# Linear attention and a two-layer perceptron on one core: the second layer of two token tiles as seven block products

## Chip, core, metric

The kernel runs on one NeuronCore of a Trainium2 chip. The metric is the device time of one execution in microseconds, as the median of several runs of the same program; smaller is better. Beside the times there is one profiled execution, whose trace gives start and duration of the instructions of each engine: TensorE (PE for matrix products, PEld for the loads of their stationary operand), VectorE (DVE), ScalarE (ACT), GpSimd (POOL) and SyncE (SP, which here only issues DMAs).

## What is computed

Batch 8, 8 heads, sequence 576, head width 64: 4608 tokens of width 512. The attention has no score matrix: softmax of q over the head width, softmax of k over the sequence, then two small products. The result is the input of two dense layers with a leaky rectifier between them.

```
q_s = softmax(q, over head width);  k_s = softmax(k, over the sequence)
kv  = einsum('bhsd,bhse->bhde', k_s, v)
x   = einsum('bhsd,bhde->bhse', q_s, kv)   -> 4608 x 512
h   = x @ w_in                             (512 x 2048)
g   = maximum(0.01 * h, h)
out = g @ w_out                            (2048 x 512), float32
```

## The kernel before

**Tiles.** The 4608 tokens are cut into nine token tiles of 512 (`NT = 9`, `TT = 512`). `xT` holds x transposed (bf16), `w_in_sb` and `w_out_sb` hold the two weights in bf16 with 128 rows of the summed index on the partitions. The order of all instructions is written out by hand; each engine works through its own list in order.

**One token tile t = 1 to 8 (lines 866 to 890).** First layer: for each of the 16 blocks j of 128 hidden channels, `layer1` (line 562) makes four matmuls with a moving operand of 512 tokens into one PSUM bank `ph`, and `leaky` (line 571) turns the bank on ScalarE into a bf16 tile `gj`. Second layer: for each of the four groups `tsub` of 128 tokens, `layer2` (line 583) makes 16 matmuls, one for each j, with a stationary block of 128 x 128 of `gj` and a moving operand of 512 columns of `w_out_sb`, all summed in one bank `pout`. `store` (line 575) copies the bank to `out_sb` (ScalarE for tiles up to 7, VectorE in tile 8) and issues two DMAs of 64 rows each from SP (line 580). The last group of tile 8 is made in two parts of 384 and 128 columns, and of each part one of the two DMAs is issued from ScalarE's queue.

**PSUM.** `psB_pool` has six banks under one tag, used in turn by `ph` and others; `psO_pool` has two for `pout`.

**Work around it.** Attention for batch b + 1 is prepared on VectorE, ScalarE, GpSimd and by DMAs while tile b is multiplied. It is hung into the loops by hooks: `at(t, u, fn)` notes it, `run(t, u)` emits it, with u below 16 for the blocks j of the first layer and 16 + 4 tsub + j // 4 for the second layer. The last attention work, that of batch 7, is emitted at (6, 23). So tiles 7 and 8 have nothing but the two layers. The SBUF pools of the attention (`raw`, `ke`, `qe`, `mx`, `small`, `qT`) stay allocated to the end, though.

**Start.** `wake` (line 370) makes a few matmuls on float32 zeros, `k_max_pe` (line 381) a transposition and `k_all_pe` (line 396) small products in float32, all within the first 12 us. They are the only float32 matmuls of the program.

Of the kernel before, what the change touches and what calls it, by code (L numbers as in the profile page):

```python
# [7 lines left out]

FP32 = mybir.dt.float32
BF16 = mybir.dt.bfloat16  # L10
AF = mybir.ActivationFunctionType
ALU = mybir.AluOpType
AX = mybir.AxisListType
# [6 lines left out]
L = 64  # L20
# [5 lines left out]
def kernel(  # L26
# [9 lines left out]
    nc = tc.nc  # L36
# [3 lines left out]
    B, H, S, D = q.shape  # L40
    C = H * D
    T = B * S
    Cm, F = moe_w_in.shape
    F2, O = moe_w_out.shape
    assert Cm == C and F2 == F and L * R == S and HL * 2 == H

    P = 128
    NB = C // P
    NF = F // P
    TT = 512  # L50
    NT = T // TT
# [3 lines left out]
    const_pool = ctx.enter_context(tc.tile_pool(name="const", bufs=1))  # L55
    w_pool = ctx.enter_context(tc.tile_pool(name="wts", bufs=1))
    xT_pool = ctx.enter_context(tc.tile_pool(name="xT", bufs=1))
    raw_pool = ctx.enter_context(tc.tile_pool(name="raw", bufs=6))
    ke_pool = ctx.enter_context(tc.tile_pool(name="ke", bufs=2))
    qe_pool = ctx.enter_context(tc.tile_pool(name="qe", bufs=2))  # L60
    mx_pool = ctx.enter_context(tc.tile_pool(name="mx", bufs=1))
    small_pool = ctx.enter_context(tc.tile_pool(name="small", bufs=3))
    qT_pool = ctx.enter_context(tc.tile_pool(name="qT", bufs=2))
    g_pool = ctx.enter_context(tc.tile_pool(name="gsb", bufs=10))
    osb_pool = ctx.enter_context(tc.tile_pool(name="osb", bufs=4))

    psB_pool = ctx.enter_context(tc.tile_pool(name="psB", bufs=6, space=bass.MemoryType.PSUM))
    psO_pool = ctx.enter_context(tc.tile_pool(name="psO", bufs=2, space=bass.MemoryType.PSUM))
    BANK_TAG = "bank2k"
# [30 lines left out]
    nc.gpsimd.memset(zero, 0.0)  # L100
    ident = const_pool.tile([P, P], BF16)
    make_identity(nc, ident)
    identf = const_pool.tile([P, P], FP32)
    make_identity(nc, identf)
    warm = const_pool.tile([P, 1], BF16)
    nc.scalar.activation(out=warm, in_=ident[:, 0:1], func=AF.Exp)
    gate = const_pool.tile([P, 1], FP32)

    w_in_sb = w_pool.tile([P, NB, F], BF16)
    w_out_sb = w_pool.tile([P, NF, O], BF16)  # L110
    xT = xT_pool.tile([P, NB, T], BF16)


    XH, X8, XE = (slice(0, 7), slice(9, 16)), slice(7, 9), slice(16, 20)
    qe1 = const_pool.tile([P, XE.stop, P], BF16, name="qe1")
    vb2 = [const_pool.tile([P, R, 2, 2, D + 2], BF16, name=f"vb{i}") for i in range(2)]
# [85 lines left out]
    def k_exp(b, hs):  # L202
        nc.scalar.activation(  # L203
            out=st[b]["ke"][:, :, hs].rearrange("p r h d -> p h r d"),
            in_=st[b]["k"][:, hs],
            func=AF.Exp,
        )
# [36 lines left out]
    def q_first(b, rs):  # L244
# [3 lines left out]
        for gg in range(2):  # L248
# [5 lines left out]
            for h in range(2):  # L254
                for r in range(n):
                    nc.scalar.activation(
                        out=st[b]["qe"][:, rs.start + r, 2 * gg + h],
                        in_=st[b]["q"][:, 2 * gg + h, rs.start + r],
                        func=AF.Exp,
                        bias=nmax[:, 2 * gg + h, r : r + 1],  # L260
# [47 lines left out]
    def q_exp(b, rs, hs=ALLH):  # L308
        nc.scalar.activation(  # L309
            out=q_cols(b, rs, hs).rearrange("p r h d -> p h r d"),  # L310
            in_=st[b]["q"][:, hs, rs],
            func=AF.Exp,
        )
# [140 lines left out]
    def q_keep(eng, b, r0, n, gs=slice(0, 4)):  # L454
        o, i = st[b]["qT"][:, gs, r0 : r0 + n], st[b]["ps", r0][:, gs]
        if eng is nc.scalar:
            eng.copy(out=o, in_=i)
        else:
            eng.tensor_copy(out=o, in_=i)
# [100 lines left out]
    def layer1(j, ph, c0, n, part=slice(0, 4), first=True, last=True):  # L560
        for cb in range(NB)[part]:
            nc.tensor.matmul(  # L562
                ph,
                lhsT=w_in_sb[:, cb, j * P : (j + 1) * P],
                rhs=xT[:, cb, c0 : c0 + n],
                start=(cb == 0 and first),
                stop=(cb == NB - 1 and last),
            )

    def leaky(o, ph):  # L570
        nc.scalar.activation(out=o, in_=ph, func=AF.Prelu, alpha=LEAKY_SLOPE)  # L571

    out_r = out.rearrange("(b l r) o -> b r l o", b=B, r=R)

    def store(row0, pout, copy=nc.vector.tensor_copy, os=slice(0, O), issue=(nc.sync, nc.sync)):
        out_sb = osb_pool.tile([P, O], FP32, name="out_sb")[:, os]
        copy(out=out_sb, in_=pout)  # L577
        for i in range(2):
            b, c = divmod(row0 + i * L, S)
            issue[i].dma_start(out=out_r[b, c // L, :, os], in_=out_sb[i * L : (i + 1) * L])  # L580

    def layer2(pout, g_sb, tsub, j, os=slice(0, O)):
        nc.tensor.matmul(  # L583
            pout,
            lhsT=g_sb[j // 2][:, j % 2, tsub * P : (tsub + 1) * P],
            rhs=w_out_sb[:, j, os],
            start=(j == 0),
            stop=(j == NF - 1),
        )
# [4 lines left out]
    def at(t, u, *fns):  # L594
        while t > 0 and u >= 32:
            t, u = t + 1, u - 32
        hooks.setdefault((t, u), []).extend(fns)

    def run(t, u):
        for fn in hooks.pop((t, u), ()):  # L600
            fn()
# [161 lines left out]
    for t in range(3, B - 1):  # L763
        b = t + 1
# [11 lines left out]
            at(t, 5, lambda b=b: load_all(b + 2))  # L776


    def g_tiles():
        return [g_pool.tile([P, 2, TT], BF16, name="gj") for _ in range(NF // 2)]  # L780

    g_sb = g_tiles()

    def begin(js, parts):
# [16 lines left out]
    def end_act(j, ph, half):  # L801
# [4 lines left out]
    t2 = (  # L806
        lambda: q_transpose(0, 6, 2, psO_pool, "pout"),
        lambda: q_keep(nc.vector, 0, 6, 2),
    )
# [38 lines left out]
    for j in range(0, NF, 2):  # L848
        if j == 0:
            ph = ahead  # L850
        else:
            ph = psB_pool.tile([P, 2, 256], FP32, name="ph", tag=BANK_TAG)
            end_pe(j, ph, 1, slice(0, 4), True)
        end_act(j, ph, 1)
    pout = [psO_pool.tile([P, O], FP32, name="pout", tag="pout") for _ in range(2)]
# [8 lines left out]
        store(tsub * P, pout[tsub])  # L864

    for t in range(1, NT):
        g_sb = []
        for j in range(NF):
            ph = psB_pool.tile([P, TT], FP32, name="ph", tag=BANK_TAG)
            layer1(j, ph, t * TT, TT)  # L870
            if j % 2 == 0:
                g_sb.append(g_pool.tile([P, 2, TT], BF16, name="gj"))
            leaky(g_sb[j // 2][:, j % 2], ph)
            run(t, j)
        for tsub in range(NTS):
            row0 = t * TT + tsub * P
            if row0 == T - P:
                for os, copy in ((slice(0, 384), nc.scalar.copy), (slice(384, O), nc.vector.tensor_copy)):
                    po = psB_pool.tile([P, os.stop - os.start], FP32, name="pout2", tag=BANK_TAG)
                    for j in range(NF):  # L880
                        layer2(po, g_sb, tsub, j, os)
                    store(row0, po, copy, os, (nc.sync, nc.scalar))
                break
            po = psO_pool.tile([P, O], FP32, name="pout", tag="pout")
            for j in range(NF):
                layer2(po, g_sb, tsub, j)
                if j == NF - 1:
                    store(row0, po, nc.scalar.copy if t < NT - 1 else nc.vector.tensor_copy)
                if j % 4 == 3:
                    run(t, 16 + 4 * tsub + j // 4)  # L890
    assert not hooks, list(hooks)
# [30 lines left out]
```

## Time and profile before

| what | value |
|---|---|
| time, median of 3 runs | 281.36 us (281.27 to 281.75) |
| span of the profiled execution, first to last instruction | 279.3 us |
| PE busy | 272.3 us, 97% of the span |
| PEld busy | 133.1 us, 48% |
| DVE, ACT, POOL busy | 158.4, 159.6 and 49.5 us |
| granted TensorE clock | 1.000 |
| HBM read, written | 36.70 MB, 9.44 MB |

The runs give the time of whole executions; the profiled execution's own time is its span and a little around it that the trace does not show: 281.36 - 279.3 = 2.1 us if it ran like the median run. A line of a profile gives source line, engine, operation, the tiles written and read, shape and type, count, then busy time in us and the mean duration of one instruction in ns. Starts and durations in a timeline are in us from the first instruction. The duration of a matmul includes the way through the array, which the next matmul does not wait for: the spacing of matmuls in a row is read from starts, not from durations.

### The profile page before, as it was taken

The page shows a single profiled execution, that of the slowest core. Times are in us where ns is not written, and L with a number is a line of the kernel's source. Part 1 is how long each engine was busy: PE and PEld are TensorE (multiplying, and loading weights), DVE is VectorE, ACT ScalarE, POOL GpSimd, SP SyncE. Part 2 cuts the span into 40 slices and gives each one's busy share as a digit, 9 for nine tenths or more (in the row PEclk, how much of TensorE's full clock was granted, in tenths as well). Part 3 has the DMA queues.
Part 4 walks back from the last instruction along what each step waited for, and adds up shares of the span by engine and source line. Part 5 has one row for each costly group of instructions (what it writes and reads, how often), then busy time and mean ns, then how long its engine had stood idle before and what let it go on. Part 6 is the DMA issues. An engine that isn't in the chain of part 4 may idle for free.

```text
span 279.3 us, 4849 instructions
## 1 busy us (share of the span) xinstructions
PE 272.3 (97%) x1927; PEld 133.1 (48%) x1954; DVE 158.4 (57%) x228; ACT 159.6 (57%) x283; POOL 49.5 (18%) x55
## 2 busy tenths in 40 slices
PE   8999999999999999999999999999999999999994
PEld 3488644444444454445444544454444444444443
DVE  3986986999999949957794688543700000000021
ACT  4977573783598458744675458644844464146400
POOL 2957460258003004000400140000000000000000
PEclk9999999999999999999999999999999999999999
DMA  7999999977993696099309930333033300330033
GB/s 253 326 209 325 246 242 306 403 269 200 300 410 139 116 405 227 2 307 361 78 9 311 347 77 2 84 77 75 1 87 75 75 1 2 75 75 0 2 75 75
DMA packets 40006, 46.45 MB, mean 166 GB/s; under 512 B 18736, under 2 KB 23344, under 8 KB 39984
## 3 DMA queue, kind: packets, MB, share of 16 engines
q1 hardware_dynamic: 36320, 41.82, 48.3%
q0 software_dynamic: 3504, 4.20, 8.7%
q8 instruction: 15, 0.25, 0.3%
q10 hardware_dynamic: 160, 0.13, 0.2%
q14 instruction: 7, 0.06, 0.1%
HBM read 36.70 MB, written 9.44 MB: 165 GB/s over the span
## 4 chain that ended last, share of the span: by engine, by line
PE 93%; DVE 3%; DMA 2%; issue 1%; ACT 0%; SPq 0%; ACTq 0%
PE pout L583 44%; PE ph L562 44%; DMA k_raw<-in_k_dram 2%; PE po L476 2%; DVE t L157 1%; PE pokv L338 1%; PE pkv L338 1%; PE pkv L416 0%; DVE k_raw L407 0%; ACT ke L203 0%; ACT gj L571 0%; DVE kmax L157 0%; DVE kd L431 0%; DVE kr L391 0%; PE pokv L476 0%
## 5 line engine op out<-in xcount | busy, mean ns | idle before, releaser
L583 PE MATMUL pout<-w_out_sb,gj 128*128 128x512 bf16 (+2 forms) x574 | 126.3, 373 | 1.2 <-issue 0.3
L562 PE MATMUL ph<-xT,w_in_sb 128*128 128x512 bf16 (+1 forms) x631 | 126.1, 357 | 0.5
L571 ACT ACTIVATE gj<-ph 128x512 bf16<-128x512 f32 x144 | 82.2, 601 | 26.0 <-PE ph L562 25.1
L562 PEld LDWEIGHTS <-w_in_sb 128*128 128x128 bf16 x640 | 62.3, 98 | 62.1 <-issue 0.2
L583 PEld LDWEIGHTS <-gj 128*128 128x128 bf16 x592 | 56.5, 98 | 65.6 <-issue 0.2
L577 ACT COPY out_sb<-pout 128x512 f32<-128x512 f32 (+1 forms) x29 | 16.8, 580 | 68.3 <-PE pout L583 43.1
L577 DVE COPY out_sb<-pout 128x512 f32<-128x512 f32 (+1 forms) x8 | 4.8, 637 | 70.8 <-PE pout L583 70.8
L215 POOL CAST vb<-v_raw 128x1152 bf16<-128x1152 f32 x13 | 21.1, 1650 | 81.4 <-DMA v_raw<-in_v_dram 81.4
L318 DVE TENSOR_REDUCE qsum<-qe 128x36 f32<-128x2304 bf16 (+5 forms) x13 | 20.0, 1542 | 10.5 <-ACT qe L309 10.4
L203 ACT ACTIVATE ke<-k_raw 128x2304 bf16<-128x2304 f32 (+2 forms) x13 | 18.0, 1384 | 8.4 <-DVE k_raw L195 8.0
L325 DVE TENSOR_TENSOR qe<-qe,qrec 128x2304 bf16<-128x2304 bf16 (+5 forms) x13 | 21.5, 1657 | 0.5
L242 DVE TENSOR_REDUCE qmax<-q_raw 128x36 f32<-128x2304 f32 (+5 forms) x13 | 20.0, 1539 | 0.1
L309 ACT ACTIVATE qe<-q_raw 128x2304 bf16<-128x2304 f32 (+5 forms) x13 | 17.1, 1315 | 4.3 <-POOL q_raw L301 3.4
L195 DVE TENSOR_TENSOR k_raw<-k_raw,kall 128x1152 f32<-128x1152 f32 (+2 forms) x10 | 18.0, 1820 | 0.3
L301 POOL TENSOR_TENSOR q_raw<-q_raw,qmax 128x512 f32<-128x512 f32 (+3 forms) x7 | 11.8, 1682 | 20.6 <-DMA q_raw<-in_q_dram 13.8
L499 ACT CAST xT<-po 128x448 bf16<-128x448 f32 (+3 forms) x34 | 14.4, 515 | 1.1 <-PE po L476 1.1
L301 DVE TENSOR_TENSOR q_raw<-q_raw,qmax 128x2304 f32<-128x2304 f32 (+1 forms) x6 | 14.0, 2332 | 0.2
L157 DVE TENSOR_TENSOR t<-t 128x256 f32<-128x256 f32 (+2 forms) x22 | 13.2, 599 | 0.7
L358 DVE RECIPROCAL krec<-pokv 128x2 f32<-128x2 f32 x8 | 1.3, 166 | 21.3 <-PE pokv L476 21.3
L157 DVE TENSOR_TENSOR t<-k_raw 128x512 f32<-128x512 f32 (+1 forms) x11 | 11.2, 1016 | 1.2 <-DMA k_raw<-in_k_dram 1.0
L370 PE MATMUL pout<-zero 128*128 128x512 f32 (+3 forms) x18 | 9.6, 659 | 1.0 <-POOL zero L100 1.0
L338 PEld LDWEIGHTS <-ke 64*64 64x64 bf16 x504 | 5.9, 107 | 3.4 <-issue 3.0
(68 smaller groups left out, 105.3 us busy)
## 6 DMA issues: line engine op xcount, KB each, us to landing
out_dram<-out_sb SPq DMA_DIRECT2D x70, 128.0 KB, 2.6
q_raw<-in_q_dram SPq DMA_DIRECT2D x6, 1152.0 KB, 8.8
v_raw<-in_v_dram SPq DMA_DIRECT2D x6, 1152.0 KB, 11.5
k_raw<-in_k_dram SPq DMA_DIRECT2D x5, 1152.0 KB, 6.2
k_raw<-in_k_dram SPq DMA_DIRECT2D x6, 576.0 KB, 6.1
v_raw<-in_v_dram SPq DMA_DIRECT2D x4, 576.0 KB, 7.6
w_in_sb<-in_moe_w_in_dram POOLq DMA_DIRECT2D x7, 256.0 KB, 7.0
w_out_sb<-in_moe_w_out_dram POOLq DMA_DIRECT2D x6, 256.0 KB, 9.3
```

The costliest lines, as they stand in the source:

```text
L157: nc.vector.tensor_tensor(out=o, in0=i0, in1=i1, op=ALU.max)
L195: eng.tensor_tensor(out=ks, in0=ks, in1=st[b]["kall"][:, hs].unsqueeze(2).to_broadcast([P, n, R, D]), op=ALU.subtract,)
L203: nc.scalar.activation(out=st[b]["ke"][:, :, hs].rearrange("p r h d -> p h r d"), in_=st[b]["k"][:, hs], func=AF.Exp,)
L215: eng.tensor_copy(out=o, in_=i)
L242: nc.vector.tensor_reduce(out=o, in_=st[b]["q"][:, hs, rs], axis=AX.X, op=ALU.max)
L301: eng.tensor_tensor(out=qs, in0=qs, in1=st[b]["qmax", rs.start, hs.start].unsqueeze(3).to_broadcast([P, m, n, D]), op=ALU.subtract,)
L318: nc.vector.reduce_sum(out=qsum, in_=q_cols(b, rs, hs), axis=AX.X)
L325: nc.vector.tensor_tensor(out=qes if out is None else out, in0=qes, in1=st[b]["qrec", rs.start, hs.start].unsqueeze(3).to_broadcast([P, n, ...
L562: nc.tensor.matmul(ph, lhsT=w_in_sb[:, cb, j * P : (j + 1) * P], rhs=xT[:, cb, c0 : c0 + n], start=(cb == 0 and first), stop=(cb == NB - 1 ...
L571: nc.scalar.activation(out=o, in_=ph, func=AF.Prelu, alpha=LEAKY_SLOPE)
L577: copy(out=out_sb, in_=pout)
L583: nc.tensor.matmul(pout, lhsT=g_sb[j // 2][:, j % 2, tsub * P : (tsub + 1) * P], rhs=w_out_sb[:, j, os], start=(j == 0), stop=(j == NF - 1),)
```

## The change

For tiles 7 and 8 (`FAST`) the second layer is computed as a 2 x 2 block product by a scheme of Strassen's kind. The 512 tokens are cut into two halves of 256 (`M2`), the 2048 hidden channels into even and odd blocks of 128 (`N2` = 8 blocks each), the 512 outputs into two halves of 256 columns (`H2`). The plain block product needs eight products of a 256 x 1024 with a 1024 x 256 block. The new one needs seven, made of 16 matmuls with 256 moving columns each, and sums of blocks before and after:

- `late_begin`, hung at (6, 24), gives up the attention's pools and allocates the new tiles in their place (`reuse_waits="tile"`: a write to a new tile waits for whoever last used that memory). It makes the sums of weight blocks t1 to t4 (128 x 2048 each: t3 on GpSimd, the others on VectorE) and a float32r copy of the block b22 on GpSimd. float32r is a four-byte type that the matmul takes in place of float32.
- `fast_layer1` replaces the first layer's loop of these tiles. The matmuls are the same; for odd j the bank is turned by two ScalarE instructions of 256 columns, one into a bf16 tile, one into the float32r tile a22. After every fourth j the sums s1, s2, s4 (VectorE) and s3 (GpSimd) of 128 x 512 are made.
- `fast_layer2` makes the products a11 b11 and a12 b21 in bf16, and s2 t2, s3 t3, s1 t1, a22 t4 and s4 b22 with both operands in float32r. ScalarE copies the first product out; VectorE adds each of the others, read from PSUM, to a float32 sum in SBUF, eleven instructions a tile. `put` issues the output DMAs. In tile 8 (`last`) the left half of the first 256 tokens is put after the second product, the other 256 tokens after the sixth, the right half of the first 256 tokens after the seventh; there the second DMA of each pair goes through ScalarE's queue, all others through SP.

The special ending of the last group (384 and 128 columns) is gone with the old loop for these tiles.

```diff
+F32R = mybir.dt.float32r
...
-    raw_pool = ctx.enter_context(tc.tile_pool(name="raw", bufs=6))
-    ke_pool = ctx.enter_context(tc.tile_pool(name="ke", bufs=2))
-    qe_pool = ctx.enter_context(tc.tile_pool(name="qe", bufs=2))
-    mx_pool = ctx.enter_context(tc.tile_pool(name="mx", bufs=1))
-    small_pool = ctx.enter_context(tc.tile_pool(name="small", bufs=3))
-    qT_pool = ctx.enter_context(tc.tile_pool(name="qT", bufs=2))
     g_pool = ctx.enter_context(tc.tile_pool(name="gsb", bufs=10))
     osb_pool = ctx.enter_context(tc.tile_pool(name="osb", bufs=4))
+    front = ctx.enter_context(ExitStack())
+    raw_pool = front.enter_context(tc.tile_pool(name="raw", bufs=6))
+    ke_pool = front.enter_context(tc.tile_pool(name="ke", bufs=2))
+    qe_pool = front.enter_context(tc.tile_pool(name="qe", bufs=2))
+    mx_pool = front.enter_context(tc.tile_pool(name="mx", bufs=1))
+    small_pool = front.enter_context(tc.tile_pool(name="small", bufs=3))
+    qT_pool = front.enter_context(tc.tile_pool(name="qT", bufs=2))
...
+    FAST = (7, 8)
+    N2, M2, H2 = NF // 2, TT // 2, O // 2
+    E1, E2 = slice(0, H2), slice(H2, O)
+    late = {}
+    def late_begin():
+        front.close()
+        pool = ctx.enter_context(tc.tile_pool(name="late", bufs=1, reuse_waits="tile"))
+        w = w_out_sb.rearrange("p (m two) o -> p m two o", two=2)
+        b11, b12, b21, b22 = w[:, :, 0, E1], w[:, :, 0, E2], w[:, :, 1, E1], w[:, :, 1, E2]
+        for n in ("b22", "t1", "t2", "t3", "t4"):
+            late[n] = pool.tile([P, N2, H2], F32R, name=n)
+        late["b11"], late["b21"] = w[:, :, 0, E1], w[:, :, 1, E1]
+        for n in ("s1", "s2", "s3", "s4", "a22"):
+            late[n] = pool.tile([P, N2, M2], F32R, name=n)
+        for n in ("e1", "u2", "u3", "u4"):
+            late[n] = pool.tile([P, 2, H2], FP32, name=n)
+        full = lambda n: late[n].bitcast(FP32)
+        nc.gpsimd.tensor_tensor(out=late["t3"], in0=b22, in1=b12, op=ALU.subtract)
+        nc.vector.tensor_tensor(out=late["t1"], in0=b12, in1=b11, op=ALU.subtract)
+        nc.vector.tensor_tensor(out=late["t2"], in0=b22, in1=full("t1"), op=ALU.subtract)
+        nc.vector.tensor_tensor(out=late["t4"], in0=b21, in1=full("t2"), op=ALU.subtract)
+        nc.gpsimd.tensor_copy(out=late["b22"], in_=b22)
+    def fast_layer1(t):
+        even = [g_pool.tile([P, 2, TT], BF16, name="gj") for _ in range(N2 // 2)]
+        odd = [g_pool.tile([P, 4, M2], BF16, name="gj") for _ in range(N2 // 4)]
+        for j in range(NF):
+            m = j // 2
+            ph = psB_pool.tile([P, TT], FP32, name="ph", tag=BANK_TAG)
+            layer1(j, ph, t * TT, TT)
+            if j % 2 == 0:
+                leaky(even[m // 2][:, m % 2], ph)
+            else:
+                leaky(odd[m // 4][:, m % 4], ph[:, 0:M2])
+                leaky(late["a22"][:, m], ph[:, M2:TT])
+            if j % 4 == 3:
+                ms, lo = slice(m - 1, m + 1), m // 2
+                a11, a21 = even[lo][:, :, 0:M2], even[lo][:, :, M2:TT]
+                a12 = odd[m // 4][:, m % 4 - 1 : m % 4 + 1]
+                part = lambda n: late[n][:, ms]
+                read = lambda n: late[n][:, ms].bitcast(FP32)
+                nc.gpsimd.tensor_tensor(out=part("s3"), in0=a11, in1=a21, op=ALU.subtract)
+                nc.vector.tensor_tensor(out=part("s1"), in0=a21, in1=read("a22"), op=ALU.add)
+                nc.vector.tensor_tensor(out=part("s2"), in0=read("s1"), in1=a11, op=ALU.subtract)
+                nc.vector.tensor_tensor(out=part("s4"), in0=a12, in1=read("s2"), op=ALU.subtract)
+            run(t, j)
+        return (lambda m: even[m // 2][:, m % 2, 0:M2]), (lambda m: odd[m // 4][:, m % 4])
+    def fast_layer2(t, a11, a12, last):
+        of = lambda n: (lambda m: late[n][:, m])
+        def product(a, w, pool=psB_pool, tag=BANK_TAG, each=False):
+            ps = [pool.tile([P, H2], FP32, name="pp", tag=tag) for _ in range(2)] if each else None
+            if not each:
+                both = pool.tile([P, 2, H2], FP32, name="pp", tag=tag)
+                ps = [both[:, 0], both[:, 1]]
+            for i in range(2):
+                for m in range(N2):
+                    nc.tensor.matmul(
+                        ps[i],
+                        lhsT=a(m)[:, i * P : (i + 1) * P],
+                        rhs=w(m),
+                        start=(m == 0 and (each or i == 0)),
+                        stop=(m == N2 - 1 and (each or i == 1)),
+                    )
+            return ps if each else both
+        def add(o, ps, e):
+            nc.vector.tensor_tensor(out=o, in0=ps, in1=e, op=ALU.add)
+        out1, out2 = ([osb_pool.tile([P, O], FP32, name="out_sb") for _ in range(2)] for _ in range(2))
+        def put(i, half, cols, issue=(nc.sync, nc.sync)):
+            for n in range(2):
+                b, c = divmod(t * TT + half * M2 + i * P + n * L, S)
+                issue[n].dma_start(
+                    out=out_r[b, c // L, :, cols], in_=(out1, out2)[half][i][n * L : (n + 1) * L, cols]
+                )
+        pe1, pu2, pu3, pu4 = (late[n] for n in ("e1", "u2", "u3", "u4"))
+        ps = product(a11, of("b11"), psO_pool, "pout")
+        nc.scalar.copy(out=pe1, in_=ps)
+        ps = product(a12, of("b21"), psO_pool, "pout")
+        for i in range(2):
+            add(out1[i][:, E1], ps[:, i], pe1[:, i])
+            if last:
+                put(i, 0, E1)
+        add(pu2, product(of("s2"), of("t2")), pe1)
+        add(pu3, product(of("s3"), of("t3")), pu2)
+        ps = product(of("s1"), of("t1"))
+        for i in range(2):
+            add(out2[i][:, E2], ps[:, i], pu3[:, i])
+        add(pu4, ps, pu2)
+        ps = product(of("a22"), of("t4"))
+        for i in range(2):
+            add(out2[i][:, E1], ps[:, i], pu3[:, i])
+            put(i, 1, slice(0, O))
+        ps = product(of("s4"), of("b22"), psO_pool, "pout", True)
+        for i in range(2):
+            add(out1[i][:, E2], ps[i], pu4[:, i])
+            put(i, 0, E2 if last else slice(0, O), (nc.sync, nc.scalar) if last else (nc.sync, nc.sync))
+    at(6, 24, late_begin)
...
     for t in range(1, NT):
+        if t in FAST:
+            fast_layer2(t, *fast_layer1(t), t == NT - 1)
+            continue
         g_sb = []
         for j in range(NF):
             ph = psB_pool.tile([P, TT], FP32, name="ph", tag=BANK_TAG)
@@ -873,19 +983,11 @@
             leaky(g_sb[j // 2][:, j % 2], ph)
             run(t, j)
         for tsub in range(NTS):
-            row0 = t * TT + tsub * P
-            if row0 == T - P:
-                for os, copy in ((slice(0, 384), nc.scalar.copy), (slice(384, O), nc.vector.tensor_copy)):
-                    po = psB_pool.tile([P, os.stop - os.start], FP32, name="pout2", tag=BANK_TAG)
-                    for j in range(NF):
-                        layer2(po, g_sb, tsub, j, os)
-                    store(row0, po, copy, os, (nc.sync, nc.scalar))
-                break
             po = psO_pool.tile([P, O], FP32, name="pout", tag="pout")
             for j in range(NF):
                 layer2(po, g_sb, tsub, j)
                 if j == NF - 1:
-                    store(row0, po, nc.scalar.copy if t < NT - 1 else nc.vector.tensor_copy)
+                    store(t * TT + tsub * P, po, nc.scalar.copy)
                 if j % 4 == 3:
                     run(t, 16 + 4 * tsub + j // 4)
     assert not hooks, list(hooks)
```

## The prediction

> **What bounds the kernel now.** I read the page's engine shares first, then the chain that ended last, then the two tiles that change, one stage at a time.
>
> ```profile
> span 279.3 us, 4849 instructions
> PE 272.3 (97%) x1927; PEld 133.1 (48%) x1954; DVE 158.4 (57%) x228; ACT 159.6 (57%) x283; POOL 49.5 (18%) x55
> PEclk9999999999999999999999999999999999999999
> PE 93%; DVE 3%; DMA 2%; issue 1%; ACT 0%; SPq 0%; ACTq 0%
> 234.01:247.82 13.81, 13.71 (x63) 6.27 (x64) 0.00 (x0) 2.35 (x4) 0.00 (x0) 1.00 0.25 57
> 247.82:261.64 13.81, 13.76 (x64) 6.27 (x64) 0.00 (x0) 9.54 (x16) 0.00 (x0) 1.00 0.09 20
> 261.64:275.49 13.85, 13.80 (x80) 7.11 (x79) 2.08 (x3) 1.08 (x2) 0.00 (x0) 1.00 0.25 57
> ```
>
> The chain is TensorE for 93% of the span, at full granted clock. The last three rows are stages cut by me: second layer of tile 7, first layer of tile 8, second layer of tile 8 (length, then busy time of PE, PEld, DVE, ACT, POOL). PE is busy through all of them, VectorE and GpSimd almost never. One second layer is 64 loads and matmuls in 13.81 us, 0.216 us a pair. So every pair less on PE shortens the run, as long as the pair keeps its price, and the other engines have room for the sums. The question is what a pair of half the width, in float32r, costs.
>
> **Price of a pair in bf16, 256 columns.** The first tile has a stage of such pairs:
>
> ```profile
> 21.94:30.69 8.75, 8.75 (x80) 7.70 (x80) 1.00 1.13 319
> ```
>
> 80 pairs in 8.75 us are 0.109 us each, half of 0.216: the load of 128 columns is hidden even there.
>
> **Price of a pair in float32r, 256 columns.** The trace has none; the nearest rows are the float32 matmuls of the start.
>
> ```profile
> L370 PE MATMUL pout<-zero 128*128 128x512 f32 (+3 forms) x18 | 9.6, 659 | 1.0 <-POOL zero L100 1.0
> 9.29 0.48 PE L370 MATMUL pout<-zero 128*128 128x256 f32 x1
> 9.40 0.19 PEld L370 LDWEIGHTS pout<-zero 128*128 128x128 f32 x1
> 9.61 0.38 PE L370 MATMUL pout<-zero 128*128 128x256 f32 x1
> 8.38 0.39 PE L370 MATMUL pout<-zero 128*128 128x128 f32 x2
> 8.49 0.28 PE L370 MATMUL pout<-zero 128*128 128x128 f32 x1
> ```
>
> The nine calls of line 370 leave 18 records: a float32 matmul is two passes, each with a load of its own. A pass of 256 columns takes 0.21 us (the second load starts at 9.40, when the first is in the array; the second matmul starts at 9.61), twice the bf16 price. Two passes at two units are four units, as many as products of two operands that are each split in two parts. The first of them waited for its load: its record is 0.48 long, the other's 0.38, so an uncovered load of 128 float32 columns costs 0.10 us. At 8.38 and 8.49 stand two passes of 128 columns, where the matmul (half of 0.21) and the load (0.10) are equally long; they start 0.11 us apart, so a load of that length still goes beside a matmul of that length, with nothing to spare. A float32r pair of 256 columns would be just such a balance, if its moving columns pass at one unit: 0.109 of matmul over 0.10 of load.
>
> Bounds: below 0.109 (nothing speaks for a four-byte pair faster than a bf16 one), above 0.43 (both passes of float32, 2 x 0.216). Between them lie 0.21 to 0.22, if one pass goes at two units as in the row at 9.61, or if one unit has its load uncovered (0.109 + 0.10). I take **0.111**, by the row 8.38 to 8.49, because one part for each operand leaves one product of the four; that step is an inference from the count of passes, and I keep the other ends as rivals.
>
> The Trainium skill, page "FP8 and Floating Point Precision", section "TensorE Precision Notes", says that true float32 takes four passes through the array, while the reduced form reads the four bytes and cuts them to 22 bits. The rows above agree with the four; no run here shows the reduced form. The Trainium skill's page "SBUF — State Buffer", section "A bandwidth-pool intuition that's wrong (but worth ruling out)", speaks against the change: it gives TensorE's moving operand 614 GB/s, two bytes a column, partition and cycle. By that figure, as an estimate, 128 x 256 x 4 bytes need 0.213 us, and the sum would be that of the first rival below.
>
> **The sum on PE.** After the change a second layer is 2 products x 16 = 32 bf16 pairs and 5 x 16 = 80 float32r pairs: 32 x 0.1094 + 80 x 0.111 = 3.50 + 8.88 = 12.38 us. Tile 7 saves 13.81 - 12.38 = 1.43, tile 8 saves 13.85 - 12.38 = 1.47, together **2.90 us**. The first layers keep their 64 pairs.
>
> **What lies beside it.** Durations of the helpers:
>
> ```profile
> L571 ACT ACTIVATE gj<-ph 128x512 bf16<-128x512 f32 x144 | 82.2, 601 | 26.0 <-PE ph L562 25.1 <-PE pout L583 0.3
> L499 ACT CAST xT<-po 128x256 bf16<-128x256 f32 x7 | 2.4, 406 | 0.3 <-PE po L476 0.3
> L157 DVE TENSOR_TENSOR t<-k_raw 128x512 f32<-128x512 f32 x6 | 4.1, 691 | 1.2 <-DMA k_raw<-in_k_dram 1.0
> L157 DVE TENSOR_TENSOR t<-t 128x512 f32<-128x512 f32 x5 | 5.1, 1021 | 0.2
> L195 DVE TENSOR_TENSOR k_raw<-k_raw,kall 128x2304 f32<-128x2304 f32 x4 | 10.2, 2558 | 0.1
> L301 POOL TENSOR_TENSOR q_raw<-q_raw,qmax 128x512 f32<-128x512 f32 x3 | 3.1, 1041 | 14.7 <-DMA q_raw<-in_q_dram 13.8 <-DVE krec L427 0.5 <-DVE qmax L242 0.3
> L301 POOL TENSOR_TENSOR q_raw<-q_raw,qmax 128x1536 f32<-128x1536 f32 x1 | 2.8, 2762 | 0.9 <-ACT gj L571 0.9
> L359 DVE TENSOR_TENSOR kd<-pokv,krec 128x128 bf16<-128x128 f32 x8 | 2.3, 292 | 0.3
> L407 DVE TENSOR_TENSOR k_raw<-k_raw,kallp 128x576 f32<-128x576 f32 x2 | 1.4, 725 | 0.0
> ```
>
> ScalarE: two blocks j bring 0.60 + 2 x 0.41 = 1.42 us where PE takes 8 x 0.216 = 1.73. It keeps up, so the split costs nothing on PE.
>
> Sums of a tile: four groups of three VectorE instructions at 0.69 (to 1.02, the slower row) and one GpSimd at 1.04, in 13.81 us of first layer. What counts is the last group. Counted from the end of the first layer: 0.2 until ScalarE starts (as at 234.21 in the timeline, below), two halves at 0.41, then s1 and s2 at 0.69 each: s2 is whole at 2.4 us, at 3.1 with the slow row. Products one and two are in front of it, 3.50 us of PE. So the sums are covered by 0.4 to 1.1 us; without that cover they would cost up to 3 us a tile.
>
> ```profile
> 234.21 0.60 ACT L571 ACTIVATE gj<-ph 128x512 bf16<-128x512 f32 x1 [0.21 <-PE ph L562]
> 31.85 1.68 POOL L301 TENSOR_TENSOR q_raw<-q_raw,qmax 128x896 f32<-128x896 f32 x1 [0.90 <-DVE qmax L242]
> 34.05 1.35 DVE L195 TENSOR_TENSOR k_raw<-k_raw,kall 128x1152 f32<-128x1152 f32 x1
> 34.21 2.73 POOL L301 TENSOR_TENSOR q_raw<-q_raw,qmax 128x896 f32<-128x896 f32 x1 [0.68 <-DVE qmax L242]
> ```
>
> The last three rows show a cost that the durations hide: the same GpSimd instruction takes 1.68 us alone and 2.73 when it starts inside a VectorE sum of 1.35; it ends 1.54 after that sum, so it stood still until then. The Trainium skill, "SBUF — State Buffer", section "Who interferes with whom", has the rule: a VectorE instruction with two SBUF inputs and a GpSimd instruction that reads SBUF exclude each other for a whole instruction; the trace agrees (1.68 against 2.73). So I add the two engines up. `late_begin` begins near 213.5: three VectorE sums of 2048 elements at about 2.3 (scaled from the 2304 row), on GpSimd one of 3.6 (1.04 and 2.76 extended from 1536 to 2048 elements) and a copy of about 2: 12.5 us, to 226. The groups of tile 7 are ready from 224, 227.5, 231 and 235 (first layer 220.2 to 234.0) and take 3.1 in turn (1.04 + 3 x 0.69): worked off one behind the other the third ends near 235.3, and the fourth has s2 near 237.7 (1.04 + 2 x 0.69 later), or at 236.7 if GpSimd's part slips in while VectorE waits for ScalarE. The third product starts at 234.0 + 3.5 = 237.5. I take it as just covered in tile 7; tile 8 has no such backlog. Nothing else waits in these engines' lists there; the tile-6 stores are on ScalarE.
>
> Adding up products on VectorE: 0.42 us for 256 columns and 0.66 for 512 (between the rows of 128 and 576), eleven a tile: 8 x 0.42 + 3 x 0.66 = 5.3 us in 12.4. Banks come free long before their next turn. Nothing of it stands on PE.
>
> **The end.** Before:
>
> ```profile
> 272.25 0.69 DVE L577 COPY out_sb<-pout 128x512 f32<-128x512 f32 x1 [2.76 <-PE pout L583]
> 272.97 3.50 SPq L580 DMA_DIRECT2D out_dram<-out_sb  x4
> 275.69 0.29 DVE L577 COPY out_sb<-pout 128x128 f32<-128x128 f32 x1 [2.75 <-PE pout L583]
> 276.01 0.47 SPq L580 DMA_DIRECT2D out_dram<-out_sb  x1
> 46.98 3.78 SPq L580 DMA_DIRECT2D out_dram<-out_sb  x6
> out_dram<-out_sb SPq DMA_DIRECT2D x1, 32.0 KB, 2.0
> ```
>
> Call R the moment at which the last product reaches VectorE, 275.69 here; SP issues the last DMA at R + 0.32 and it lands 2.0 later. After the change the sixth product reaches VectorE 16 x 0.111 = 1.78 before R. Its first add ends at R - 1.36 and SP begins: four DMAs of the second 256 tokens, then one of each right half, six in all. Six in a row took 3.78 us, 0.6 each (0.63 with the load of that time, 0.5 and 0.6 in turn in the pair at 272.97). The sixth starts at R - 1.33 + 5 x 0.6 = R + 1.67 instead of R + 0.32. VectorE's longer add alone (0.42 against 0.29) would have made it R + 0.45. The tail grows by **1.3 us** (0.1 if SP's list were empty).
>
> **Sum:** -2.90 + 1.35 = -1.55, so the span goes from 279.3 to about 277.7. With the 2.1 us between span and median, **279.8 us**. Pairs at 0.109 give 279.5; at 0.114, 280.3; with a shorter tail, 279.2.
>
> **Rivals.**
> 1. *The float32r pair takes two units* (a pass of 256 columns as at 9.61, or an uncovered load). For it: no four-byte column in this trace moves faster than that. Against: float32's two units come in two passes that look like four products. A second layer is 3.50 + 80 x 0.216 = 20.8, 7.0 more in each tile; the products at the end are longer, SP's list empties in time and the tail grows by 0.13 only: 281.36 + 14.1 = **295.4 us**. This is the slower side. It decides early: the gain is gone when 160 pairs cost 1.55 us more, at 0.111 + 0.0097 = 0.121 us a pair. A partly uncovered load, 0.115 to 0.13, lies around that point: 280.4 to 282.9.
> 2. *float32r is multiplied like float32*, so that the change doesn't do what its type says: 0.43 a pair, 34.6 + 3.5 = 38.1 a layer, 24.3 more twice: **330 us**.
> 3. *The sums come late* (the backlog of tile 7, sums at 1.02, GpSimd in between): s2 at 3.1 + 1.04 = 4.1, product three waits 0.6 us in each tile: **281.0 us**, next to no change.
>
> **How the numbers follow.** Forecast 0.69 (own range 279.2 to 280.5); late sums 0.08; partly uncovered load 0.04; two units 0.16; four units 0.03. The range reaches from 279.2 to 283, up to the partly uncovered load; outside it are the last two cases, 0.19. A measurement here tells 0.2%, 0.56 us, from no change. Faster by more: the forecast and a little of the partly uncovered load, 0.70; within: late sums and the middle of the partly uncovered load, 0.10; slower: 0.20.
>
> **What would show it.** The five float32r products each as 16 matmuls with starts 0.111 apart, one record a call (two units: 0.216 apart; four: two records each). Second layers of 12.4 us. PE without a gap before the third product, or a wait there for VectorE's s2. The start of the last SP issue 1.6 to 1.7 us behind the last product's arrival at VectorE, with SP busy from the sixth product's first add on. If the pairs are as I say and the time is not lower, the end or the sums have taken it.

## The result, and the profile after

The changed kernel takes 281.92 us (median of 19 runs, 281.5 to 283.64), the kernel before 281.29 us (19 runs, 281.14 to 281.93) beside it: a ratio of 1.0021, 95% interval 1.0013 to 1.0029. The forecast was 279.8 us and faster.

Of the changed kernel's page: span, engines, granted clock and the chain that ended last.

```profile
span 280.1 us, 5125 instructions
PE 272.4 (97%) x2034; PEld 145.2 (52%) x2034; DVE 197.1 (70%) x273; ACT 158.8 (57%) x296; POOL 65.7 (23%) x65
PEclk9999999999999999999999999999999999999999
PE 83%; DVE 12%; DMA 2%; ACT 1%; issue 0%; SPq 0%
```

VectorE and GpSimd are busy for 39 and 16 us more, mostly with the new sums. What was not expected is in the last row: the chain now runs through VectorE for 12% of the span, up from 3%, although the block sums were to be covered. Somewhere TensorE has begun to wait for work that VectorE delivers.

The second layers of tiles 7 and 8, cut out as stages (length, then busy time of PE, PEld, DVE, ACT, POOL):

```profile
235.00:248.09 13.09, 13.09 (x113) 12.70 (x112) 6.88 (x13) 1.24 (x3) 1.15 (x1) 1.00 0.01 2
261.92:275.00 13.08, 13.08 (x113) 12.69 (x111) 6.94 (x13) 1.24 (x3) 1.15 (x1) 1.00 0.09 24
```

13.09 and 13.08 us in place of 13.81 and 13.85: 1.49 us saved, half of the 2.90 forecast. PE is busy throughout, so no wait for the sums eats it. PEld points at where the rest may be: it is busy for 12.7 of 13.1 us, where it had 6.3 of 13.8 before. The matmuls of tile 7 by product, in the order of time (start, time to the end of the last one, count):

```profile
235.00 3.66 PE L840 MATMUL pp<-w_out_sb,gj 128*128 128x256 bf16 x32
238.42 6.00 PE L840 MATMUL pp<-t,s 128*128 128x256 f32 x48
244.25 2.08 PE L840 MATMUL pp<-t,a 128*128 128x256 f32 x16
246.17 2.08 PE L840 MATMUL pp<-b,s 128*128 128x256 f32 x16
```

The 16 pairs of a22 t4 take from 244.25 to 246.17: 0.120 us each, one record a call. The 32 bf16 pairs take 0.109. float32r is one pass at nearly the bf16 rate, and the third product follows the second without a gap; but a pair is 11 ns dearer than bf16, not 2.

The end (VectorE's last adds, the output DMAs of SP and ScalarE):

```profile
273.28 0.76 DVE L850 TENSOR_TENSOR out_sb<-pp,u 128x256 f32<-128x256 f32 x2 [0.56 <-PE pp L840]
273.73 3.95 SPq L857 DMA_DIRECT2D out_dram<-out_sb  x6
275.19 0.42 DVE L850 TENSOR_TENSOR out_sb<-pp,u 128x256 f32<-128x256 f32 x1 [0.53 <-PE pp L840]
277.14 0.55 SPq L857 DMA_DIRECT2D out_dram<-out_sb  x1
```

The last add begins at 275.19 and SP's sixth DMA at 277.14, 1.95 us behind it; before, SP's last issue stood 0.32 us behind VectorE's last copy. Between the start of the last matmul and the end of the span lie 5.24 us (274.88 to 280.12) against 3.88 (275.44 to 279.32): the tail is 1.36 us longer.

That leaves a loss that no term of the forecast has. Tile 7's first layer begins at 221.19 us where it began at 220.20 before (first row after, second row before):

```profile
221.19 0.38 PE L564 MATMUL ph<-xT,w_in_sb 128*128 128x512 bf16 x1
220.20 1.03 PE L562 MATMUL ph<-xT,w_in_sb 128*128 128x512 bf16 x4
```

The step in it stands at 184.74 (two rows after, then the same two before):

```profile
182.56 2.12 ACT L205 ACTIVATE ke<-k_raw 128x2304 bf16<-128x2304 f32 x1 [4.65 <-DVE k_raw L197]
184.74 0.38 PE L340 MATMUL pokv<-vb,ke 64*64 64x65 bf16 x24 [0.55 <-ACT ke L205]
```

```profile
178.73 2.12 ACT L203 ACTIVATE ke<-k_raw 128x2304 bf16<-128x2304 f32 x1 [1.19 <-DVE k_raw L195]
183.74 0.38 PE L338 MATMUL pokv<-vb,ke 64*64 64x65 bf16 x24
```

In batch 7's attention TensorE waits 0.55 us for ke (the exponentials of k). ScalarE made ke 3.8 us later than before (182.56 against 178.73), having waited for VectorE. Followed back on VectorE and GpSimd, after and then before:

```profile
164.32 4.93 POOL L799 TENSOR_TENSOR t<-w_out_sb 128x2048 fp32r<-128x2048 bf16 x1
169.19 2.36 POOL L803 CAST b<-w_out_sb 128x2048 fp32r<-128x2048 bf16 x1
165.35 6.47 DVE L159 TENSOR_TENSOR t<-t 128x512 f32<-128x512 f32 x2
```

```profile
164.97 1.15 DVE L157 TENSOR_TENSOR t<-t 128x512 f32<-128x512 f32 x2
```

GpSimd made t3 and the copy of b22 at 164 to 171.5 us, fifty microseconds ahead of the place where `late_begin` stands for TensorE. Its list held nothing that kept it back. While it worked, VectorE's maxima of k (two SBUF inputs) took 6.47 us in place of 1.15, so some 5 of VectorE's 39 us more are standing still. The chain from k to ke to TensorE had less than that to spare. The profiled span adds up: -1.49 for the layers, +1.36 for the tail, +0.99 for the late start of tile 7 is +0.86, and 280.1 - 279.3 is 0.8. Of the 0.99, 0.38 was there by 100 us already, long before any new instruction runs; run 4 looks at it.

### The profile page after: what moved, and what is told of

Its sections match the earlier page's. It is cut to its first block, busy times and chain, and to the rows that moved or that the text cites. A ratio compares the mean times of both kernels' runs of the same rounds, so it can differ in the third digit from the quotient of the medians.

```text
span 280.1 us, 5125 instructions
## 1 busy us (share of the span) xinstructions
PE 272.4 (97%) x2034; PEld 145.2 (52%) x2034; DVE 197.1 (70%) x273; ACT 158.8 (57%) x296; POOL 65.7 (23%) x65
## 4 chain that ended last, share of the span: by engine, by line
PE 83%; DVE 12%; DMA 2%; ACT 1%; issue 0%; SPq 0%
PE ph L564 39%; PE pout L585 30%; PE pp L840 9%; DVE t L159 4%; DMA k_raw<-in_k_dram 2%; PE po L478 2%; DVE q_raw L303 1%; PE pokv L340 1%; ACT ke L205 1%; DVE k_raw L197 1%; DVE qe L327 1%; DVE qsum L320 1%; DVE qmax L244 1%; PE pkv L340 1%; PE pkv L418 0%; DVE k_raw L409 0%
## 5 line engine op out<-in xcount | busy, mean ns | idle before, releaser
L585 PE MATMUL pout<-w_out_sb,gj 128*128 128x512 bf16 x448 | 99.6, 379 | 0.0
L573 ACT ACTIVATE gj<-ph 128x512 bf16<-128x512 f32 (+1 forms) x144 | 78.8, 578 | 36.6 <-PE ph L564 35.5
L585 PEld LDWEIGHTS <-gj 128*128 128x128 bf16 x448 | 43.0, 98 | 51.1 <-issue 0.2
L579 ACT COPY out_sb<-pout 128x512 f32<-128x512 f32 x24 | 13.9, 584 | 40.7 <-PE pout L585 19.3
L823 POOL TENSOR_TENSOR s<-gj 128x512 fp32r<-128x512 bf16 x8 | 9.2, 1153 | 82.4 <-DMA out_dram<-out_sb 53.1
L824 DVE TENSOR_TENSOR s<-gj,a 128x512 fp32r<-128x512 bf16 x8 | 6.8, 853 | 25.4 <-ACT a L573 25.4
L159 DVE TENSOR_TENSOR t<-t 128x256 f32<-128x256 f32 (+2 forms) x22 | 17.8, 808 | 0.7
L159 DVE TENSOR_TENSOR t<-k_raw 128x512 f32<-128x512 f32 (+1 forms) x11 | 12.1, 1102 | 0.9 <-DMA k_raw<-in_k_dram 0.8
L840 PE MATMUL pp<-t,s 128*128 128x256 f32 x96 | 12.0, 284 | 0.0
```

The costliest lines, as they stand in the source:

```text
L159: nc.vector.tensor_tensor(out=o, in0=i0, in1=i1, op=ALU.max)
L585: nc.tensor.matmul(pout, lhsT=g_sb[j // 2][:, j % 2, tsub * P : (tsub + 1) * P], rhs=w_out_sb[:, j, os], start=(j == 0), stop=(j == NF - 1),)
L840: nc.tensor.matmul(ps[i], lhsT=a(m)[:, i * P : (i + 1) * P], rhs=w(m), start=(m == 0 and (each or i == 0)), stop=(m == N2 - 1 and (each or ...
```

## The experiments

**1. GpSimd held back.** A copy of one column, which reads what the attention wrote last, stands in front of its two instructions.

```diff
+        nc.gpsimd.tensor_copy(out=gate[:, 0:1], in_=xT[:, 0, T - 1 : T])
         nc.gpsimd.tensor_tensor(out=late["t3"], in0=b22, in1=b12, op=ALU.subtract)
```

> GpSimd's two instructions on the weight blocks (t3 and the copy of b22) are made to wait, by a one-column copy in front of them that reads the last tokens of xT, so that they can't run before the attention is through. Theory: in the changed kernel they ran at 164 to 171.5 us and kept VectorE out, and TensorE stood 0.55 us for ke; so here the maxima of line 159 take 1.2 us in place of 6.5, the wait for ke is gone, and the time is 0.6 us under the changed kernel's 281.9: 281.3. Rival: the long maxima are covered and the kernel before lacks the wait for another reason; then the time stays at 281.9.

Measured: 281.11 us, 281.18 before (ratio 0.9998, 0.9990 to 1.0007). Against the kernel before it stands 0.70 us better than the changed kernel did (-0.07 in place of +0.63). VectorE, ScalarE, TensorE and GpSimd in its trace:

```profile
164.11 1.98 DVE L159 TENSOR_TENSOR t<-t 128x512 f32<-128x512 f32 x2
178.64 2.12 ACT L205 ACTIVATE ke<-k_raw 128x2304 bf16<-128x2304 f32 x1 [1.18 <-DVE k_raw L197]
183.66 0.38 PE L340 MATMUL pokv<-vb,ke 64*64 64x65 bf16 x24
215.92 4.06 POOL L800 TENSOR_TENSOR t<-w_out_sb 128x2048 fp32r<-128x2048 bf16 x1 [0.34 <-POOL gate L799]
```

The wait for ke is gone: the group at 183.66 has no idle time in front, and stood at 183.74 in the kernel before. So the theory holds, but for one number: the maxima take 1.98 us and not 1.2. Beside them GpSimd's cast of v ran until 165.08:

```profile
162.94 2.14 POOL L217 CAST vb<-v_raw 128x1152 bf16<-128x1152 f32 x1
```

**2. The last DMAs shared between two queues.**

```diff
-            put(i, 1, slice(0, O))
+            put(i, 1, slice(0, O), (nc.sync, nc.scalar) if last else (nc.sync, nc.sync))
```

> Of the second 256 tokens' four output DMAs of the last tile, two go through ScalarE's queue in place of SP's. Theory: the tail is SP's list of six; the last SP issue starts 0.45 us behind the last add's start in place of 1.94, and the time falls by 1.3 to 1.5 us, from 281.9 to 280.5. Rival: the tail is set by the transfers themselves (three quarters of a megabyte in the last 4 us), which don't get less; then it falls by under 0.4 us.

Measured: 280.87 us, 281.18 before (0.9989, 0.9980 to 0.9998): 0.94 us better against its kernel before than the changed kernel. More than the rival's 0.4, less than the theory's 1.3.

```profile
273.52 2.40 SPq L857 DMA_DIRECT2D out_dram<-out_sb  x4
273.53 2.68 ACTq L857 DMA_DIRECT2D out_dram<-out_sb  x4
274.99 0.42 DVE L850 TENSOR_TENSOR out_sb<-pp,u 128x256 f32<-128x256 f32 x1 [0.53 <-PE pp L840]
```

Each queue now has four issues in 2.4 and 2.7 us. SP's last one starts 0.45 us behind the last add, as the theory had it. The last of all starts 0.99 us behind the last matmul, on ScalarE's queue, which I had taken to be free by then; in the kernel before that distance was 0.58. The tail is 4.42 us, against 5.24 in the changed kernel and 3.88 before. So SP's list of issues was the larger part of the loss, and of the 0.54 us that are left, the later last issue makes up 0.41.

**3. The sums in bf16.** Both pools of sums become `BF16`, and the bitcasts go.

```diff
-            late[n] = pool.tile([P, N2, H2], F32R, name=n)
+            late[n] = pool.tile([P, N2, H2], BF16, name=n)
...
-            late[n] = pool.tile([P, N2, M2], F32R, name=n)
+            late[n] = pool.tile([P, N2, M2], BF16, name=n)
```

> All sums of blocks (s1 to s4, t1 to t4, a22, b22) are held in bf16 in place of float32r, nothing else is changed; the sums are rounded more. Theory: the 160 pairs of the five products fall from 0.120 to 0.109 us, second layers from 13.08 to 12.24 us, the time by 1.7 us to 280.2. Rival: 0.120 belongs to operands that were just written by VectorE, or to the waits between products, and not to the four-byte load; then the pairs stay at 0.115 to 0.120 and the time at 281.3 or more.

Measured: 279.95 us, 281.18 before (0.9956, 0.9943 to 0.9968), 1.86 us better against before than the float32r version. The same products in its trace:

```profile
238.20 5.40 PE L840 MATMUL pp<-t,s 128*128 128x256 bf16 x48
243.44 1.91 PE L840 MATMUL pp<-t,a 128*128 128x256 bf16 x16
245.19 1.91 PE L840 MATMUL pp<-b,s 128*128 128x256 bf16 x16
```

243.44 to 245.19 are 0.109 us a pair. 160 x 11 ns are 1.8 us. The operands are just as fresh and the order of the products the same, so the 0.120 belongs to the type.

**4. The pools alone.** The kernel before with the pools in the changed order.

> The kernel before with nothing but the order of the pools in SBUF as in the changed kernel; no block products. Theory: addresses cost nothing, 281.3 us as before, and the 0.38 us by which the changed kernel is late at 100 us is scatter of a profile. Rival: the moved pools are slower to reach; then 281.6 to 281.7, with the same 0.3 to 0.4 us late by 100 us.

Measured: 281.08 us, 281.18 before (1.0002, 0.9989 to 1.0016). Its trace, and those of the three runs above, which have the pools and the new code too, stand within 0.15 us of the kernel before at 100 us. So the 0.38 us was scatter of one profile: over all traces of this document the first product of batch 4's attention begins between 100.24 and 101.05 us (100.43 before, 100.81 in the changed kernel). The loss in batch 7's attention can be read free of it. From that product in batch 6 to that in batch 7 it is 28.92 us before and in run 1, and 29.55, 29.65 and 29.57 in the changed kernel and in runs 2 and 3, which don't hold GpSimd back.

**5 and 6. Both repairs, in float32r and in bf16.** The edits of 1 and 2 together, then those of 1, 2 and 3.

> Both repairs of the float32r version: GpSimd's weight sums held back, and two of the last tile's DMAs moved to ScalarE's queue. Theory: they add up, 281.9 - 0.6 - 1.4 = 279.9 us, faster than the kernel before by 0.5%: what is left is the saving of the two second layers, 1.5 us. Rival: held back, GpSimd and VectorE collide with tile 7's sums and the third product waits; then 280.3 or more, with a wait of TensorE for s2.

> As the run before it, and the sums of blocks held in bf16, which rounds them more. Theory: pairs at 0.109, 1.7 us less again: 278.2 us. Rival: as with bf16 alone, 279.9.

Measured: 280.22 us in float32r (0.9966, 0.9952 to 0.9979) and 278.61 in bf16 (0.9910, 0.9897 to 0.9924), with 281.14 before. The second layers of the bf16 version (length, then busy time of PE, PEld, DVE, ACT, POOL):

```profile
233.97:246.20 12.23, 12.23 (x113) 10.96 (x112) 6.08 (x13) 1.25 (x3) 1.15 (x1) 1.00 0.00 0
260.01:272.25 12.24, 12.24 (x113) 10.87 (x111) 6.14 (x13) 1.25 (x3) 1.15 (x1) 1.00 0.09 23
```

The float32r version is at -0.92, and its parts say the same: -1.49 for the layers, +0.59 for its tail of 4.47 us. It is 0.3 us above its theory, which had reckoned with 1.4 us from the queues where run 2 gave 0.94. The bf16 version is at -2.53: two layers at 12.24 us in place of 13.81 and 13.85 save 3.18, its tail of 4.57 costs 0.69. Both are faster than the kernel before, and the bf16 version rounds its sums more. In neither does TensorE wait for s2, so GpSimd's late work does not hold up tile 7's sums.

**7 to 10. What the eleven nanoseconds are.** All four hold GpSimd back, and change the form of the matmuls in `product` alone. Each leaves out or mixes up part of the sums, so the spacing of matmuls is what is read from them, not their times (one execution each: 277.03, 282.82, 280.19 and 282.97 us for runs 7, 8, 9 and 10).

> GpSimd held back; and in all seven products the moving operand is cut from 256 to 128 columns for 14 of the 16 matmuls, so half of the outputs of these tiles are not summed up. Theory: a float32r pair is bound by its load; its spacing stays at 0.11 to 0.12 us though the matmul is half as long, while the bf16 pairs fall to 0.056. Rival: the load is covered and the moving columns set the 0.120 (0.47 ns a column); then float32r pairs fall to 0.06.

> GpSimd held back; and in all seven products the stationary block is cut from 128 to 64 columns for 12 of the 16 matmuls, so half of the token rows of these tiles are not summed up. Theory: with a load half as long the matmul of 256 columns sets the spacing: 0.109 us in float32r as in bf16. Rival: the moving columns or a fixed cost of the type set it: 0.117 to 0.120.

> GpSimd held back; and in six of the seven products each stationary block is multiplied with 512 moving columns (two blocks of the right side beside each other), 8 matmuls of 512 in place of 16 of 256, so that the blocks are summed in a wrong way. Measures what a float32r matmul costs by itself. Theory: the price over bf16 is the coupling of load and matmul, some 6 to 11 ns a pair whatever its width: 0.222 to 0.227 us against 0.216 in bf16. First rival: four-byte columns pass slower, 0.115 / 256 = 0.45 ns each: 0.230 us. Second rival: with a matmul twice as long as the load nothing is left: 0.216.

> GpSimd held back; and the stationary block cut to 32 columns for 12 of 16 matmuls, so that three quarters of the token rows of these tiles are not summed up. With 64 columns the float32r pairs stood at 0.113 to 0.117. Theory: that is what a 256-column float32r matmul costs with its load hidden, so 32 columns change nothing: 0.113 to 0.117. Rival: what is left over 0.109 still comes of the load and shrinks with it: 0.110 to 0.112.

Run 7:

```diff
+                    n = H2 if m == 0 else P
-                        ps[i],
+                        ps[i][:, 0:n],
...
-                        rhs=w(m),
+                        rhs=w(m)[:, 0:n],
```

Run 8 (run 10 has 32 in place of 64):

```diff
+                    n = P if m in (0, N2 - 1) else 64
-                        ps[i],
-                        lhsT=a(m)[:, i * P : (i + 1) * P],
+                        ps[i][0:n],
+                        lhsT=a(m)[:, i * P : i * P + n],
```

Run 9:

```diff
-                for m in range(N2):
+                for m in range(0, N2, 1 if each else 2):
...
-                        ps[i],
+                        ps[i] if each else both,
...
-                        rhs=w(m),
+                        rhs=w(m) if each else w(slice(m, m + 2)),
...
-                        stop=(m == N2 - 1 and (each or i == 1)),
+                        stop=(m == N2 - (1 if each else 2) and (each or i == 1)),
```

Two rows of each trace, a22 t4 and s4 b22 in tile 7; from start to start is the time of the first. Run 7, half the moving columns (the form shown is that of the first matmul; in front of them six cut bf16 pairs):

```profile
234.30 0.50 PE L842 MATMUL pp<-w_out_sb,gj 128*128 128x128 bf16 x6
241.54 1.96 PE L842 MATMUL pp<-t,a 128*128 128x256 f32 x16
243.34 1.96 PE L842 MATMUL pp<-b,s 128*128 128x256 f32 x16
```

Run 8, half the load (in front three cut bf16 pairs), then run 10, a quarter of it:

```profile
235.19 0.49 PE L842 MATMUL pp<-w_out_sb,gj 128*64 128x256 bf16 x3
244.59 2.02 PE L842 MATMUL pp<-t,a 128*128 128x256 f32 x16
246.44 2.02 PE L842 MATMUL pp<-b,s 128*128 128x256 f32 x16
```

```profile
244.56 2.05 PE L842 MATMUL pp<-t,a 128*128 128x256 f32 x16
246.45 2.05 PE L842 MATMUL pp<-b,s 128*128 128x256 f32 x16
```

Run 9, twice the moving columns, eight matmuls in the first row:

```profile
242.95 1.98 PE L841 MATMUL pp<-t,a 128*128 128x512 f32 x8
244.76 2.07 PE L841 MATMUL pp<-b,s 128*128 128x256 f32 x16
```

| run | columns moved | columns loaded | us a pair, mean of the row |
|---|---|---|---|
| changed kernel | 256 | 128 | 0.120 |
| 7 | 128 | 128 | 0.113 |
| 8 | 256 | 64 | 0.116 |
| 10 | 256 | 32 | 0.118 |
| 9 | 512 | 128 | 0.227 |

(The means of 7, 8 and 10 hold a few full matmuls. The cut ones alone stand at 0.110 to 0.115 mostly, 0.113 to 0.118 and 0.115 to 0.119. For the cut bf16 pairs the last one's record is taken off: 0.50 - 0.22 are five steps of 0.056 in run 7, 0.49 - 0.27 two steps of 0.109 in run 8.)

In run 7 the load sets the pace, as the theory said: half the matmul, yet 0.113 in place of the bf16 pairs' 0.056. But run 8 goes against the theory: with half the load the pair should have come down to 0.109, and it stands at 0.116; a quarter of the load (run 10) brings it down no further. In both traces the bf16 pairs with the same cut loads settle at 0.109, so what is left over 0.109 belongs to the type. (Where the loaded width changes, one bf16 matmul follows another only after 0.20 us; inside the float32r products no such step is seen. By it tile 7's two bf16 products last 4.3 us in runs 8 and 10 in place of 3.5.) Run 9 puts 0.227 against 0.216 in bf16: 11 ns again at twice the width, at the upper end of the theory's range and under the first rival's 0.230.

So a float32r load needs about 0.113 us a time, a float32r matmul 7 to 11 ns more than a bf16 one, and side by side they take 0.120. Neither covers the other fully. What makes the matmul dearer, these runs don't settle. A fixed price of 9 to 11 ns a matmul fits runs 9 and 10. A price by the column fits as well: 0.227 / 512 is 0.443 ns a column, which makes 0.113 of 256 columns, the shortest spacing in run 8.

**11 and 12. One DMA for 128 rows.** In the last tile the two DMAs of 64 rows become one whose target has the shape 2 x 64 x columns.

```diff
+            if last:
+                b, c = divmod(t * TT + half * M2 + i * P, S)
+                issue[0].dma_start(out=out_r[b, c // L : c // L + 2, :, cols], in_=(out1, out2)[half][i][:, cols])
+                return
...
-            put(i, 0, E2 if last else slice(0, O), (nc.sync, nc.scalar) if last else (nc.sync, nc.sync))
+            put(i, 0, E2 if last else slice(0, O), (nc.scalar if last and i == 0 else nc.sync, nc.sync))
```

> Sums of blocks in bf16, GpSimd held back, and in the last tile one output DMA for 128 rows in place of two for 64, the first right half through ScalarE, all others through SP. Theory: the tail is SP's list; half as many issues leave it empty, the last issue starts 0.6 us behind the last matmul as in the kernel before, the tail is 3.9 to 4.0 us in place of 4.57, and the time is 278.0 us (278.6 with the issues shared out). Rival: a DMA of 256 KB takes as much longer; 278.6 or more.

> The same with the sums in float32r. Theory: 280.2 - 0.5 = 279.7 us, 1.5 us under the kernel before: the whole saving of the two second layers at 0.120 us a pair, and nothing lost at the end. Rival: 280.2.

Measured: 293.12 us (1.0428, 1.0414 to 1.0442) and 294.77 (1.0488, 1.0474 to 1.0502), 281.02 before. Both sides were far off. The end of run 11 (queues, then stages with the DMA engines' mean share and GB/s in the last two columns):

```profile
270.99 5.98 SPq L858 DMA_DIRECT2D out_dram<-out_sb  x3
271.87 1.13 ACTq L858 DMA_DIRECT2D out_dram<-out_sb  x1
```

```profile
276.00:280.00 4.00, 0.00 (x0) 0.00 (x0) 0.00 (x0) 0.00 (x0) 0.00 (x0) 0.56 0.13 50
284.00:289.00 5.00, 0.00 (x0) 0.00 (x0) 0.00 (x0) 0.00 (x0) 0.00 (x0) 0.50 0.13 50
```

The end of the changed kernel for comparison:

```profile
276.00:279.50 3.50, 0.00 (x0) 0.00 (x0) 0.00 (x0) 0.00 (x0) 0.00 (x0) 1.00 0.57 156
```

The issues are fewer, and each transfer crawls: 50 GB/s at a DMA share of 0.13, as much as two engines of sixteen, where the changed kernel's end has 156 GB/s at 0.57. The outer dimension of the target is two here. The Trainium skill, "DMA: Bandwidth & Descriptors", section "Rules for kernel authors", has it that an outermost dimension below 16 confines a DMA to at most that many engines, and the trace agrees (0.13 of sixteen is 2.1). As a test of the tail these runs say nothing; the idea needs a shape with the 64 rows outside, which wasn't tried.

## Why the prediction was wrong, point by point

**The step that failed** is "I take 0.111, by the row 8.38 to 8.49". The pair measures 0.120, and bf16 sums (run 3) give the difference back. The row was a single interval between two passes of one float32 matmul, of 128 columns; "with nothing to spare" was the right reading and should have been priced as a range, not as a point at its good end. One pass and close to one unit a column were right, and neither two nor four units came. What failed is the overlap: the forecast lets the load go beside the matmul for 2 ns, and a load of 0.113 us (run 7) and a matmul of 0.116 to 0.118 (runs 8 and 10) take 0.120 together. So the term was mis-sized, 2.90 us forecast and 1.49 measured. The break-even that the first rival names, 0.121, was hit almost exactly. Its case of a "partly uncovered load, 0.115 to 0.13" (280.4 to 282.9 us) holds the result, and I gave it 0.04. Two things about that are luck or half right: at 0.120 the forecast's own sum comes to 281.2 us, and the other 0.7 come from the step below; and most of the excess stays when the load is halved or quartered.

**The step that was left out.** "`late_begin` begins near 213.5" put GpSimd's instructions at TensorE's place in the program. But GpSimd ran ahead in its own list: its last cast of v ended at 164.2 us, and with nothing to wait for it began t3 at 164.32. The exclusion of the two engines, which the forecast had priced for tile 7 only, struck batch 7's attention instead, for 0.6 to 0.7 us (run 1). The Trainium skill, "SBUF — State Buffer", section "Who interferes with whom", has the rule, and the trace agrees once more: 6.47 us in place of 1.15. The sums for tile 7 themselves were covered, with 1.0 us to spare before the third product where the forecast had "just covered"; by 210.7 us both engines were through with the weight sums.

**Right in its mechanism, with some luck in its size:** the tail. Forecast +1.35 us from SP's list of six; measured +1.36, and run 2 takes 0.82 of it away. The agreement to 0.01 is luck: the sixth issue stands 1.95 us behind the last add's start, not 1.67, but from the last issue to the end of the span it is 2.98 us where it was 3.30 before. Right too: ScalarE's split, the banks, no wait for s2, bf16 pairs at 0.109.

The 614 GB/s that the Trainium skill's page "SBUF — State Buffer" gives for TensorE's moving operand ("A bandwidth-pool intuition that's wrong (but worth ruling out)") would make, as an estimate, 0.213 us of a float32r pair; the trace has 0.120, so it doesn't bound four-byte columns here. The Trainium skill's page "FP8 and Floating Point Precision", section "TensorE Precision Notes", has a reduced form beside the four passes of true float32 but no count of its passes; the traces have one record a float32r call.

With 1.49 saved, 1.36 lost at the end and 0.6 to 0.7 in the attention, the kernel comes out 0.5 to 0.6 us slower; measured 0.63.

## What to carry to other kernels

A saving of 5% in two short stages, here 1.49 us, is spent by a tail of 1.36 us: count the DMA issues that become due after the last matmul before counting products. When load and matmul are equally long, price the pair by a run of many, and ask what it costs if neither hides. And work that is placed late in the program must be tied to something late, or an engine with an empty list will do it early, in the way of others.

## What the runs showed of the hardware that I had not expected

A float32r pair of 256 columns costs 0.120 us, and 0.116 to 0.118 when its load is cut to a half or a quarter, against 0.109 in bf16. A float32r load of 128 columns takes about 0.113 us, where bf16 pairs with the same load went by every 0.056 us (run 7). Joined output DMAs with an outer dimension of two ran at 50 GB/s, as much as two of sixteen engines, and made the tail 19 us long in place of 4.5.
